# Queries and keys of a head pair in one load, and new places for the work: decay attention with a routed expert layer

## The chip, the core and the metric

The kernel runs on one core of a Trainium2 chip. A core has five engines with queues of their own: TensorE (PE, with its weight loads shown apart as PEld), VectorE (DVE), ScalarE (ACT), GpSimd (POOL) and SyncE (SP), which here only issues transfers; sixteen DMA engines do the moving. The metric is device time in microseconds (us) of one execution. Before the change three executions took 407.04, 410.15 and 414.75 us, a median of 410.15.

## The reference

Eight batches of eight heads, 576 positions, 64 numbers per head. The first stage is causal attention with a decay made of cumulated gates `f`; the second sends the 128 best-scored rows of each batch through a two-layer expert network and adds the result to them.

```python
def _attn_ref(q, k, v, f):
    scale = 1.0 / np.sqrt(D)
    scores = scale * np.matmul(q, k.transpose(0, 1, 3, 2))
    cum = np.cumsum(np.log(np.clip(f, 0.0001, 1.0)), axis=-1)
    decay = cum[:, :, :, None] - cum[:, :, None, :]
    scores = np.where(causal, -1000000000.0, scores + decay)
    attn = np.exp(scores - np.max(scores, axis=-1, keepdims=True))
    attn = attn / (np.sum(attn, axis=-1, keepdims=True) + 1e-09)
    return np.matmul(attn, v)

def _moe_ref(x, w_gate, w1, w2, capacity):          # x: (8, 576, 512), capacity 128
    scores = np.einsum('bsd,d->bs', x, w_gate)
    out = x.copy()
    for b in range(B):
        top_idx = np.argpartition(-scores[b], capacity)[:capacity]
        xe = x[b, top_idx]
        ye = np.maximum(xe @ w1, 0.0) @ w2
        g = 1.0 / (1.0 + np.exp(-scores[b, top_idx]))
        out[b, top_idx] = x[b, top_idx] + g[:, None] * ye
    return out
```

## The kernel before, in words

The 64 heads are worked in 32 pairs, two heads on the two halves of the 128 partitions. For a pair `p`:

- SyncE loads the keys of both heads (`rk`, 288 KB, one transfer, line 535) and the queries (`rq`, three transfers of 144, 128 and 16 KB, lines 540 to 542). The queries of the second head stand in another order: the last 64 first, then the others, and the first 64 of that second part are repeated at the end, so that any block of 128 columns can be taken as weights. A row of the decay (`e`, 288 KB, broadcast from DRAM) is loaded for each head (line 556) and the values (`v`, four transfers, line 606).
- GpSimd makes masked copies `m` of `e` (line 455). TensorE makes the scores of five groups of columns ("scores", line 644); VectorE adds `m` or `e` and takes the row's extreme in the same instruction (line 688); ScalarE takes the exponential (line 736); TensorE turns the result block by block ("transposes", line 755), and the turned blocks are copied out of PSUM into `pt` (line 382 on ScalarE, line 386 on VectorE); TensorE multiplies `pt` with `v` ("output products", line 838); the result is copied to `both` (the same lines 382 and 386), turned back (line 902) and normed on VectorE (line 907).
- At the end of four pairs a batch is stored, its 128 rows are selected (lines 1049, 1057, 1081), gathered by GpSimd (line 1093) and multiplied with the two layers on TensorE ("expert products", lines 1164, 1171, 1223, 1231); GpSimd scatters the rows back (line 1242).

Two kinds of copy can go to either engine. The last four copies into `pt` of a pair (blocks of 64x256, 128x256, 64x256 and 128x128) go to VectorE for the pairs in the list `ON_H`, else to ScalarE. The copy of 128x448 into `both` goes to VectorE for the pairs in `ON_O`, else to ScalarE.

The order on each engine is fixed when the program is built: a planner (class `Flow`) keeps a clock for each engine, takes the ready step that can start first, and breaks ties by the step's `place`, a number made of the constants that stand at the head of the kernel function. Every engine then runs its list in that order. A step also takes buffers: three `raw` buffers for keys and three `rq` buffers for queries, so a pair's load waits until TensorE is through with the scores of the pair three before. The transfers of SyncE use eight semaphores in turn (`DMAHW0` to `DMAHW7`), and each transfer waits at its issue for the one that used its semaphore before: at most eight are under way.

## Time and profile before

| what | value |
|---|---|
| median of 3 executions | 410.15 us (407.04 to 414.75) |
| the profiled execution's own time | 406.7 us |
| its span, first to last instruction | 405.0 us |
| TensorE busy (matmul) | 385.0 us, 95% |
| TensorE weight loads busy | 263.9 us, 65% |
| VectorE busy | 300.7 us, 74% |
| ScalarE busy | 314.0 us, 78% |
| GpSimd busy | 208.4 us, 51% |
| bytes moved | 68.06 MB, mean 168 GB/s |

The span and busy times are of one profiled execution, 3.4 us under the median of the three runs. Busy shares are means over very different stretches: a fill of some 60 us in which transfers are dense, a middle in which all engines work, and a tail of expert products from 359 us on with TensorE nearly alone.

### The profile page before, as it was taken

Reading aid. Unit: us, or ns where it says so; the run is one execution under the profiler, and the core shown is the slowest. Engines: PE = TensorE matmul, PEld = TensorE weight load, DVE = VectorE, ACT = ScalarE, POOL = GpSimd, SP = SyncE. Lnnn points to the kernel's source line nnn. Section 1 sums busy time; section 2 is a strip of 40 time slices with the busy share of each in tenths; the row PEclk is TensorE's granted clock in tenths of the full one; section 3 lists DMA queues with packets and bytes.
Section 4 is the critical chain, followed back from the end, with each engine's and each line's share of the span. In section 5 each row is a group of like instructions: output and inputs, shape, how many; then the busy total and the mean of one; then the engine's idle time right before and its main releaser. Section 6 shows DMA issues by size and latency. Waiting matters only on the chain.

```text
span 405.0 us, 11830 instructions
## 1 busy us (share of the span) xinstructions
PE 385.0 (95%) x3979; PEld 263.9 (65%) x3979; DVE 300.7 (74%) x1147; ACT 314.0 (78%) x971; POOL 208.4 (51%) x355
## 2 busy tenths in 40 slices
PE   8689898999989999999999999999999999999994
PEld 6475566656565666666675767757576657767773
DVE  3837889797995799899479963889879797278401
ACT  4979799989988998789999885689988798512220
POOL 5873778959495955337542641556453644031201
PEclk9959999999999999999999999999999999999998
DMA  5889799779888965658675651668556333011101
GB/s 146 250 212 236 197 268 247 214 204 247 239 201 260 255 182 157 201 150 246 165 203 156 177 174 45 177 200 223 159 169 187 93 120 109 34 58 54 54 0 52
DMA packets 74306, 68.06 MB, mean 168 GB/s; under 512 B 45155, under 2 KB 54406, under 8 KB 74246
## 3 DMA queue, kind: packets, MB, share of 16 engines
q1 hardware_dynamic: 72886, 62.97, 56.9%
q0 software_dynamic: 1280, 4.20, 3.0%
q8 instruction: 31, 0.51, 0.5%
q14 instruction: 29, 0.24, 0.2%
q10 hardware_dynamic: 80, 0.15, 0.1%
HBM read 55.59 MB, written 11.70 MB: 166 GB/s over the span
## 4 chain that ended last, share of the span: by engine, by line
PE 57%; DMA 12%; issue 11%; DVE 9%; ACT 6%; POOL 2%; SPq 1%; POOLq 0%; ACTq 0%; DVEq 0%
PE banks L644 15%; PE banks L838 15%; PE banks L755 8%; PE banks L1164 6%; PE banks L1223 5%; DVE p L688 4%; DMA v<-in_v_dram 4%; ACT p L736 3%; DMA rq<-in_qk_dram 3%; PE banks L1171 2%; DMA e<-eq 2%; PE banks L1231 2%; PE banks L902 2%; DMA xe<-out_dram,idx 2%; ACT pt L382 2%
## 5 line engine op out<-in xcount | busy, mean ns | idle before, releaser
L736 ACT ACTIVATE p<-p,nm 128x320 f32<-128x320 f32 (+4 forms) x288 | 166.4, 585 | 10.7 <-DVE nm L688 9.6
L455 POOL TENSOR_SCALAR_AFFINE_SELECT m<-e 128x320 f32<-128x320 f32 (+3 forms) x256 | 109.6, 457 | 83.6 <-DMA e<-eq 46.5
L382 ACT COPY pt<-banks 128x256 f32<-128x256 f32 (+4 forms) x296 | 111.8, 439 | 21.7 <-PE banks L755 20.4
L644 PE MATMUL banks<-rk,rq 64*128 64x192 f32 (+4 forms) x768 | 114.3, 417 | 3.5 <-DMA rq<-in_qk_dram 1.4
L688 DVE CUSTOM_DVE_ANT_0 p<-banks,m 64x64 f32<-64x64 f32 (+3 forms) x256 | 101.6, 418 | 12.8 <-PE banks L644 8.3
L838 PE MATMUL banks<-pt,v 128*64 128x448 f32 (+4 forms) x768 | 93.2, 392 | 0.1
L644 PEld LDWEIGHTS banks<-rk,rq 64*128 64x128 f32 x768 | 67.8, 190 | 22.5 <-DVE nm L688 6.4
L755 PEld LDWEIGHTS banks<-ident,p 64*128 64x128 f32 x1472 | 61.2, 141 | 27.3 <-issue 8.3
L838 PEld LDWEIGHTS banks<-pt,v 128*64 128x64 f32 x768 | 45.8, 137 | 47.5 <-issue 31.7
L755 PE MATMUL banks<-ident,p 64*128 64x64 f32 x1472 | 69.7, 230 | 6.9 <-ACT pt L382 4.0
L916 POOL TENSOR_TENSOR gj<-x,wg 128x640 f32<-128x640 f32 x32 | 49.9, 1568 | 35.0 <-DVE x L907 18.2
L736 ACT ACTIVATION_READ_ACCUMULATOR p<-p,nm 128x1 f32 x288 | 56.5, 196 | 0.0
L688 DVE CUSTOM_DVE_ANT_0 p<-banks,e 128x384 f32<-128x384 f32 x64 | 34.5, 552 | 14.0 <-PE banks L644 13.3
L1049 DVE SCALAR_TENSOR_TENSOR j<-srow,sg,later 128x576 uint8<-128x576 f32 (+1 forms) x40 | 33.0, 826 | 0.8
L907 DVE TENSOR_TENSOR x<-banks,rn 128x640 f32<-128x640 f32 x32 | 25.6, 816 | 9.8 <-PE banks L902 8.6
L688 DVE DVE_READ_ACCUMULATOR2_ANT nm<- 128x1 f32 (+1 forms) x384 | 31.0, 81 | 0.0
L1242 POOL DMA_INDIRECT out_dram<-xe,idx x8 | 8.7, 1086 | 40.7 <-DVE xe L1238 35.8
L921 DVE TENSOR_REDUCE gu<-gj 128x5 f32<-128x640 f32 x32 | 25.6, 813 | 4.8 <-POOL gj L916 4.8
L688 DVE CUSTOM_DVE_ANT_0 p<-banks,m,nm 128x192 f32<-128x192 f32 x64 | 26.4, 413 | 3.1 <-PE banks L644 2.3
L1223 PE MATMUL banks<-w2h,hth 128*128 128x512 f32 x64 | 27.2, 425 | 0.2 <-ACT hth L1204 0.2
L1164 PE MATMUL banks<-w1h,xth 128*128 128x512 f32 x64 | 27.0, 423 | 0.0
L1177 ACT ACTIVATE h<-banks 128x512 f32<-128x512 f32 x16 | 9.4, 596 | 22.0 <-PE banks L1171 19.8
(87 smaller groups left out, 389.9 us busy)
## 6 DMA issues: line engine op xcount, KB each, us to landing
e<-eq SPq DMA_DIRECT2D x62, 288.0 KB
rk<-in_qk_dram SPq DMA_DIRECT2D x32, 288.0 KB
out_dram<-x SPq DMA_DIRECT2D x16, 512.0 KB
rq<-in_qk_dram SPq DMA_DIRECT2D x32, 144.0 KB
rq<-in_qk_dram SPq DMA_DIRECT2D x32, 128.0 KB
v<-in_v_dram SPq DMA_DIRECT2D x32, 128.0 KB
v<-in_v_dram SPq DMA_DIRECT2D x32, 80.0 KB
srow<-sd SPq DMA_DIRECT2D x7, 320.0 KB
```

The costliest lines, as they stand in the source:

```text
L382: nc.scalar.copy(d, s_)
L455: nc.gpsimd.affine_select(out=dst, in_=src, pattern=w, compare_op=ALU.is_ge, fill=NEG, base=base, channel_multiplier=1)
L644: nc.tensor.matmul(st["sc", u][hh][:, o:o + k1 - k0], q_rows(raws["q", p], hh, i), raws["k", p][rows, k0:k1], start=True, stop=True)
L688: nc.vector.tensor_tensor_reduce(out=into(hh, i, r_, x0, x1), in0=blocks(b_[r_, x0 - k0:x1 - k0], hh, i), in1=blocks(in1(), hh, i), scale= ...
L736: nc.scalar.activation(x, x, AF.Exp, bias=st["nm", hh, i], scale=-1.0, accum_out=l)
L755: nc.tensor.transpose(tp[:, g, col:col + R], src, ident[g * R:g * R + R, g * R:g * R + R])
L838: nc.tensor.matmul(avb[p, g][par * D:(par + 1) * D, qo + q0 - g * SPL:qo + q1 - g * SPL], vt[:, j, par * D:(par + 1) * D], pt[:, off:off + ...
L907: nc.vector.tensor_tensor(out=xhs[key][:, :, w_ * P:(w_ + 1) * P].rearrange("p c (h d) -> p c h d", h=2), in0=st["tb"][:, :, 0:NCH * D].re ...
L916: (nc.vector if e == "dve" else nc.gpsimd).tensor_tensor(out=gjs[p % 2], in0=xhs[key][:, :, w0:w1], in1=wg[:, hb * HB + w0:hb * HB + w1].u ...
L1049: nc.vector.scalar_tensor_tensor(junk[0:n, :], st["srow"][0:n, 0:S], sg()[0:n, c:c + 1], later[0:n, o:o + S], ALU.subtract, ALU.is_gt, acc ...
L1164: nc.tensor.matmul(q["hp", n][0:nr, :], q["xth"][:, c, 0:nr], r_[:, c, cs], start=(c == 0 and k_ == 0), stop=False)
L1223: nc.tensor.matmul(q["yp"][0:nr, :], q["hth"][:, c, 0:nr], r_[:, c, :], start=(c == 0 and k_ == 0), stop=False)
```

## The change

Keys and queries of a pair are loaded by one transfer of 576 KB into one `raw` buffer of 1216 columns (queries, then 64 columns, then keys), and a second transfer of 16 KB repeats the first 64 queries of the second head's reordered row behind them. The `rq` buffers and the three memsets that cleared a corner of them are gone; the corner now holds the last 64 queries, which no result uses. The lists of copies on VectorE grow, `ON_H` from 6 to 15 pairs and `ON_O` from 14 to 19, and most of the planner's constants have other values. The number and the shapes of TensorE's instructions are the same.

```diff
-    ON_H = (2, 4, 6, 15, 23, 27)
-    ON_O = (0, 1, 2, 3, 4, 5, 7, 9, 12, 18, 21, 23, 29, 30)
-    BD = 18.628
+    ON_H = (0, 1, 2, 3, 5, 10, 12, 13, 14, 19, 21, 24, 25, 26, 30)
+    ON_O = (0, 1, 3, 4, 5, 8, 10, 12, 13, 14, 18, 20, 21, 22, 24, 25, 26, 29, 30)
+    BD = 17.596
...
-    PR = -837.457
-    PL = -228.901
-    PS = 1729.975
+    PR = -648.646
+    PL = -211.77
+    PS = 1838.312
...
     QW = S + R
-    RQ = 3
-    rqs = [const.tile([P, QW], F32, name=f"rq{r}") for r in range(RQ)]
...
-    def t_zero(e):
-        for t in rqs:
-            (nc.vector if e == "dve" else nc.gpsimd).memset(t[D:P, 0:R], 0.0)
-
-    d_zero = add({"dve": 0.4}, t_zero, place=-70)
-
...
-        tk = tks[p] = {"q": Token("rq", 4), "k": Token("raw", 4)}
-
-        def t_k(e):
-            t = raws["k", p] = rawp.tile([P, S], F32, tag="raw", name=f"rk{p}")
-            src = qk[2 * p:2 * p + 2, :, 1, :].rearrange("h d s -> (h d) s")
-            nc.sync.dma_start(out=t, in_=src)
-
-        def t_q(e):
-
-            t = raws["q", p] = rqs[p % RQ]
-            nc.sync.dma_start(out=t[0:D, 0:S], in_=qk[2 * p][:, 0, :])
-            nc.sync.dma_start(out=t[D:P, R:S], in_=qk[2 * p + 1][:, 0, R:S])
+        tk = tks[p] = {"k": Token("raw", 4)}
+
+        def t_qk(e):
+            t = raws[p] = rawp.tile([P, QW + S], F32, tag="raw", name=f"qk{p}")
+            x = t[:, 0:1]
+            nc.sync.dma_start(out=bass.AP(t.tensor, x.offset, [x.ap[0], [QW, 2], [1, S]]), in_=qk[2 * p:2 * p + 2].rearrange("h d g s -> (h d) g s"))
             nc.sync.dma_start(out=t[D:P, S:QW], in_=qk[2 * p + 1][:, 0, 0:R])
 
-        lk = load(t_k, 288, after=[st_eq] * (p > 1), place=pl, take=[tk["k"]])
-        lq = load(t_q, 288, 3, after=[d_zero] + [st_eq] * (p > 1), place=pl + 0.1, take=[tk["q"]])
-
-        ops[p] = [lk, lq]
+        lk = load(t_qk, 592, 2, after=[st_eq] * (p > 1), place=pl, take=[tk["k"]])
+
+        ops[p] = [lk]
...
-                        nc.tensor.matmul(st["sc", u][hh][:, o:o + k1 - k0], q_rows(raws["q", p], hh, i), raws["k", p][rows, k0:k1],
+                        nc.tensor.matmul(st["sc", u][hh][:, o:o + k1 - k0], q_rows(raws[p], hh, i), raws[p][rows, QW + k0:QW + k1],
                                          start=True, stop=True)
```

Because every place is new, instructions move on all engines. Three spots matter below; in the rows a name's first number is the pair (`rk2`, `rq2` and `qk2` are pair 2's, except that `rq` counts its three buffers) and `nm1_2_1` belongs to pair 1.

SyncE in the fill, before: twelve transfers after the keys of pair 2 have been issued (the wait in brackets is the semaphore of the transfer eight places ahead, and the engines that must be through with the buffer).

```order
L556 DMA e0_89<-eq_79 128x576 [waits DMAHW4_49,DVE_49,Pool_49]
L556 DMA e1_90<-eq_79 128x576 [waits DMAHW5_49,DVE_49,Pool_49]
L606 DMA v2_115<-in_v_dram 128x4x64 [waits DMAHW6_49]
L606 DMA v2_115<-in_v_dram 64x64 [waits DMAHW7_49]
L606 DMA v2_115<-in_v_dram 64x5x64 [waits DMAHW0_49]
L606 DMA v2_115<-in_v_dram 64x4x64
L931 DMA wg_85<-in_w_gate_dram 128x512 [waits DMAHW2_49]
L973 DMA wst0_305<-in_w1_dram 128x1024 [waits DMAHW3_49]
L556 DMA e2_91<-eq_79 128x576 [waits DMAHW4_49,DVE_49,Pool_49]
L540 DMA rq2_88<-in_qk_dram 64x576 [waits DMAHW5_49]
L541 DMA rq2_88<-in_qk_dram 64x512 [waits DMAHW6_49]
L542 DMA rq2_88<-in_qk_dram 64x64 [waits DMAHW7_49]
```

The same spot now, from the first row of the decay that is loaded:

```order
L541 DMA e2_88<-eq_79 128x576 [waits DMAHW5_49]
L527 DMA qk2_209<-in_qk_dram 128x2x576
L528 DMA qk2_209<-in_qk_dram 64x64 [waits DMAHW0_49]
L541 DMA e1_87<-eq_79 128x576 [waits DMAHW1_49,DVE_49,Pool_49]
L541 DMA e0_86<-eq_79 128x576 [waits DMAHW2_49]
L591 DMA v2_112<-in_v_dram 128x4x64 [waits DMAHW3_49]
L591 DMA v2_112<-in_v_dram 64x64 [waits DMAHW4_49]
L591 DMA v2_112<-in_v_dram 64x5x64
L591 DMA v2_112<-in_v_dram 64x4x64 [waits DMAHW6_49]
L916 DMA wg_85<-in_w_gate_dram 128x512 [waits DMAHW7_49]
L541 DMA e2_88<-eq_79 128x576 [waits DMAHW0_49,DVE_49,Pool_49]
L958 DMA wst0_305<-in_w1_dram 128x1024 [waits DMAHW1_49]
```

The queries of pair 2 moved from behind values, gate and the first weights to ahead of them; the two decay rows `e0` and `e1` changed their order, and from the first values to the second loads into `v0` and `v1` (the last transfers before pair 6) SyncE's list has 35 rows where it had 45.

ScalarE at the end of the fill's first two pairs, before:

```order
L736 ACTIVATE p1_0_236,st1_100<-p1_0_236,nm1_0_1_319 128x576
L736 ACTIVATE p1_0_236,st1_100<-p1_0_236,nm1_1_1_335 128x320
L382 COPY pt0_116<-banks_78 64x4x64
L382 COPY pt0_116<-banks_78 128x2x128
L382 COPY pt0_116<-banks_78 64x4x64
L382 COPY pt0_116<-banks_78 128x2x64
L382 COPY pt1_117<-banks_78 128x4x128 x2
L382 COPY pt1_117<-banks_78 128x2x128 x2
L736 ACTIVATE p1_2_261,st1_100<-p1_2_261,nm1_2_1_351 128x448
```

and now:

```order
L721 ACTIVATE p1_0_226,st1_97<-p1_0_226,nm1_1_1_361 128x320
L721 ACTIVATE p1_0_226,st1_97<-p1_0_226,nm1_0_1_339 128x576
L380 COPY pt1_114<-banks_78 128x2x128 x2
L721 ACTIVATE p1_2_248,st1_97<-p1_2_248,nm1_2_1_393 128x448
L380 COPY pt1_114<-banks_78 128x4x128 x2
```

The four last copies of pair 0 left ScalarE's list here (they stand on VectorE now, between the last masks of pair 1 and the first scores of pair 2), and ScalarE comes to the exponentials of pair 1 that much sooner.

TensorE around the turning back of pairs 2 and 3, before (`both` is what it waits for, the copies of the output products):

```order
L838 MATMUL banks_78<-pt1_117,v0_113 64x192 x2
L755 MATMUL banks_78<-ident_81,p4_2_831 128x64 x16
L755 MATMUL banks_78<-ident_81,p40_97 128x64 x2
L755 MATMUL banks_78<-ident_81,p4_2_831 128x64
L755 MATMUL banks_78<-ident_81,p4_0_752 128x64
L755 MATMUL banks_78<-ident_81,p4_2_831 128x64
L755 MATMUL banks_78<-ident_81,p4_0_752 128x64
L902 MATMUL banks_78<-ident_81,both_112 128x64 x20
```

and now:

```order
L823 MATMUL banks_78<-pt1_114,v0_110 64x448 x4
L823 MATMUL banks_78<-pt1_114,v0_110 64x128 x2
L823 MATMUL banks_78<-pt1_114,v0_110 64x320 x2
L823 MATMUL banks_78<-pt1_114,v0_110 64x64 x2
L823 MATMUL banks_78<-pt1_114,v0_110 64x192 x2
L887 MATMUL banks_78<-ident_81,both_109 128x64 x20
L740 MATMUL banks_78<-ident_81,p4_0_756 128x64 x24
```

The turning back stood behind 22 transposes of pair 4; now it stands right behind the products whose copies it needs, and the transposes follow it.

## Rows read from the trace of the kernel before

**Rows 1.** The page's first part: busy time, share of the span, instructions.
```profile
PE 385.0 (95%) x3979; PEld 263.9 (65%) x3979; DVE 300.7 (74%) x1147; ACT 314.0 (78%) x971; POOL 208.4 (51%) x355
```
**Rows 2.** Four stretches: length, each engine's busy time, clock, DMA share, GB/s.
```profile
8.00:60.00 52.00, 45.54 (x483) 31.74 (x483) 36.96 (x171) 45.11 (x146) 36.01 (x65) 0.90 0.88 226
60.00:140.00 80.00, 75.80 (x922) 50.62 (x918) 66.83 (x266) 74.61 (x242) 61.14 (x96) 1.00 0.85 233
140.00:340.00 200.00, 198.05 (x2140) 132.87 (x2139) 164.57 (x640) 172.34 (x540) 95.28 (x163) 1.00 0.59 166
340.00:405.00 65.00, 59.46 (x430) 44.14 (x428) 29.16 (x62) 17.76 (x41) 12.24 (x10) 0.98 0.14 48
```
**Rows 3.** Stretches of 2 us in the fill: PE, PEld, DVE, ACT, POOL, clock.
```profile
16.00:18.00 2.00, 1.06 (x16) 0.62 (x14) 1.30 (x9) 2.00 (x7) 1.94 (x6) 1.00 0.93 185
18.00:20.00 2.00, 0.76 (x13) 0.63 (x13) 1.29 (x8) 2.00 (x10) 1.79 (x7) 0.96 0.95 292
...
24.00:26.00 2.00, 1.88 (x6) 1.46 (x8) 0.22 (x1) 1.95 (x8) 1.85 (x4) 0.50 0.75 186
26.00:28.00 2.00, 2.00 (x15) 1.71 (x12) 1.33 (x7) 0.00 (x0) 2.00 (x3) 0.50 0.95 289
...
30.00:32.00 2.00, 2.00 (x18) 1.51 (x16) 1.41 (x7) 1.98 (x8) 0.00 (x0) 0.98 0.78 175
```
**Rows 4.** Chain that ended last, in the fill: start, length, what.
```profile
11.89 4.74 DMA v<-in_v_dram
...
16.65 7.86 DMA rq<-in_qk_dram
...
38.41 6.45 DMA v<-in_v_dram
```
**Rows 5.** SyncE's queue in the fill: issue of pair 2's last query transfer.
```profile
17.32 0.60 SPq L542 DMA_DIRECT2D rq<-in_qk_dram  x1
```
**Rows 6.** TensorE in time: start, length, [idle before, and what ended it].
```profile
24.12 3.50 PE L644 MATMUL banks<-rk,rq 64*128 64x384 f32 x11 [1.35 <-DMA rq<-in_qk_dram]
...
40.16 1.02 PE L755 MATMUL banks<-ident,p 64*128 64x64 f32 x22
41.71 0.83 PE L902 MATMUL banks<-ident,both 64*128 64x64 f32 x20 [0.53 <-ACT both L382]
```
**Rows 7.** VectorE in time: pair 2's first scores, and a pair's last four copies.
```profile
25.78 0.56 DVE L688 CUSTOM_DVE_ANT_0 p<-banks,e 128x384 f32<-128x384 f32 x1 [4.61 <-PE banks L644]
...
43.09 1.48 DVE L386 COPY pt<-banks 64x256 f32<-64x256 f32 x4
```
**Rows 8.** Copies by shape: count, busy us, mean ns, idle before.
```profile
L382 ACT COPY pt<-banks 128x256 f32<-128x256 f32 x90 | 30.7, 382 | 9.1 <-PE banks L755 9.1
...
L382 ACT COPY pt<-banks 64x256 f32<-64x256 f32 x52 | 19.1, 368 | 0.9 <-PE banks L755 0.5
...
L382 ACT COPY both<-banks 128x448 f32<-128x448 f32 x18 | 9.4, 524 | 5.8 <-PE banks L838 5.8
...
L386 DVE COPY both<-banks 128x448 f32<-128x448 f32 x14 | 8.6, 618 | 5.8 <-PE banks L838 5.8
L382 ACT COPY pt<-banks 128x128 f32<-128x128 f32 x26 | 6.9, 266 | 0.4
```
**Rows 9.** TensorE in time: expert products, then transposes; two products later.
```profile
229.33 0.39 PE L1223 MATMUL banks<-w2l,hth 128*128 128x512 f32 x1
229.65 0.84 PE L755 MATMUL banks<-ident,p 64*128 64x64 f32 x19
...
231.76 0.40 PE L1223 MATMUL banks<-w2l,hth 128*128 128x512 f32 x1
232.00 0.40 PE L1223 MATMUL banks<-w2h,hth 128*128 128x512 f32 x1
```
**Rows 10.** Two stretches with dense VectorE work; columns as in Rows 2.
```profile
100.00:120.00 20.00, 19.29 (x234) 13.11 (x233) 19.44 (x79) 18.95 (x59) 14.24 (x22) 1.00 0.83 217
260.00:300.00 40.00, 39.56 (x435) 26.17 (x435) 32.88 (x131) 36.71 (x117) 18.37 (x36) 1.00 0.62 174
```

More of the change, by code (lines that the diff above doesn't have):

```diff
@@ L212 @@
     FR = 3 * R
-    ON_H = (2, 4, 6, 15, 23, 27)
-    ON_O = (0, 1, 2, 3, 4, 5, 7, 9, 12, 18, 21, 23, 29, 30)
-    BD = 18.628
+    ON_H = (0, 1, 2, 3, 5, 10, 12, 13, 14, 19, 21, 24, 25, 26, 30)
+    ON_O = (0, 1, 3, 4, 5, 8, 10, 12, 13, 14, 18, 20, 21, 22, 24, 25, 26, 29, 30)
+    BD = 17.596
     WP = 17
     WQ = 0
-    R0 = -51.187
-    X0 = -111.892
-    XE_ = -1130.192
-    XH_ = 221.862
-    XM_ = -523.148
-    XB_ = -6.884
-    XN_ = -497.454
-    XO_ = -420.006
-    XU_ = 1.418
-    XQ_ = 583.927
@@ L229 @@
-    XR_ = 438.027
-    XG_ = 433.66
-    PL4 = 226.946
-    GW = 48.938
-    EPS = 0.007
-    LOOK = 13
-    PR = -837.457
-    PL = -228.901
-    PS = 1729.975
-    PV = 419.503
-    PW_ = -377.929
-    PM = -181.961
-    PE_ = 150.687
-    PC = -338.491
-    PB = -208.409
-    PD = -36.514
-    VO = -2.178
+    R0 = -52.147
+    X0 = -124.883
+    XE_ = -1075.113
+    XH_ = 159.99
+    XM_ = -564.831
+    XB_ = -7.101
+    XN_ = -664.091
+    XO_ = -436.104
+    XU_ = 1.143
+    XQ_ = 636.004
@@ L246 @@
+    XR_ = 439.718
+    XG_ = 408.245
+    PL4 = 219.529
+    GW = 52.142
+    EPS = 0.0
+    LOOK = 13
+    PR = -648.646
+    PL = -211.77
+    PS = 1838.312
+    PV = 403.168
+    PW_ = -460.22
+    PM = -142.517
+    PE_ = 117.893
+    PC = -308.846
+    PB = -168.777
+    PD = -36.497
+    VO = -0.958
     VD = 1
     GD = 0.1
-    WS = 43.949
-    WD = 829.304
-    LL = 242.025
-    A0 = 12.159
-    A1 = 57.554
-    A2 = 19.879
-    A3 = -2.292
-    A4 = 139.495
-    A5 = 55.535
-    A6 = 49.92
@@ L258 @@
-    A7 = -229.773
-    M0 = -26.555
-    M1 = -15.965
-    M2 = -18.758
-    M3 = -36.076
-    M4 = 82.571
-    M5 = -295.763
-    M6 = 466.944
-    M7 = -52.0
-    N0 = 44.201
-    N1 = -67.418
-    N2 = -47.01
-    N3 = 1.415
-    N4 = 131.251
-    N5 = 167.057
-    N6 = 116.74
-    N7 = -261.773
-    WL = 163.972
-    RK = 88.355
-    RD = 3.183
-    XP = 14.83
-    GO = 31.138
-    GS = 2.047
-    GL = -334.287
+    WS = 118.216
+    WD = 752.615
+    LL = 304.571
+    A0 = 19.277
+    A1 = 52.87
@@ new lines @@
+    A2 = 18.506
+    A3 = 3.665
+    A4 = 209.607
+    A5 = 48.408
+    A6 = 28.379
+    A7 = -323.357
+    M0 = -31.531
+    M1 = -24.322
+    M2 = -4.752
+    M3 = -43.62
+    M4 = 62.42
+    M5 = -357.068
+    M6 = 390.929
+    M7 = -62.326
+    N0 = 56.704
+    N1 = -59.781
+    N2 = -71.8
+    N3 = -2.564
+    N4 = 159.49
+    N5 = 117.493
+    N6 = 70.124
+    N7 = -235.852
+    WL = 82.957
+    RK = 91.535
+    RD = 3.307
+    XP = 16.067
+    GO = 34.078
+    GS = 2.098
+    GL = -319.652
@@ L386, in copy_on @@
             nc.vector.tensor_copy(d, s_)
-    flow = Flow({"raw": 3, "rq": 3, "v": 3, "p0": 2, "p1": 2, "p4": 2, "pt": 2, "ot0": 1, "ot1": 1,
+    flow = Flow({"raw": 3, "v": 3, "p0": 2, "p1": 2, "p4": 2, "pt": 2, "ot0": 1, "ot1": 1,
                  "x": 2, "nm": 10, "h": 1, "hth": 1, "htl": 1, "xth": 1, "xtl": 1, "xe": 2, "srow": 1,
@@ L1091, in gd @@
             else:
-                q["xe"] = rawp.tile([P, S], F32, tag="raw", name=f"xe{b}_{rt}")[:, 0:DM]
+                q["xe"] = rawp.tile([P, QW + S], F32, tag="raw", name=f"xe{b}_{rt}")[:, 0:DM]
             nc.gpsimd.indirect_dma_start(
```

## The prediction

> **What bounds the kernel now.** I read the page's first part, then busy times by stretch, then the fill in steps of 2 us with the chain of waits, then the copies by shape. The page says TensorE 95% and no other engine over 78% [rows 1]. The stretches split that up [rows 2]. From 140 to 340 us TensorE idles 1.95 us of 200, so there only less TensorE work, or closer packing, can help. From 60 to 140 us it idles 4.20 us of 80 while ScalarE is busy 74.61 of 80: ScalarE paces. From 8 to 60 us it idles 6.46 us, the DMA engines are busy at 0.88, and the clock is 0.90 of full. The last 65 us are expert products on a full TensorE and a fixed end, and I find nothing changed there. What can be won lies before 140 us: 10.7 us of idle, and a low clock.
>
> The fill in detail. [...] Inside the low stretch stands the largest single wait that the change touches: TensorE starts the scores of pair 2 at 24.12, released by that pair's queries [rows 6]. Their last transfer was issued at 17.32 [rows 5] behind values, gate vector and weights. VectorE had idled 4.61 us by then [rows 7], and ScalarE idles the whole of 26 to 28 us [rows 3]. The chain of waits shows the same: transfers that follow one another from 11.89 to 44.86 us [rows 4].
>
> **The change, part by part.** TensorE's instructions keep number and shape. So I price the waits, the copies and the order.
>
> *Fill, transfers.* Two issues fewer per pair, and the queries of pair 2 come right behind its keys. From the first values to the last transfers before pair 6 SyncE has 35 transfers where it had 45; one of the ten is a decay row put off, so nine are really gone. Since at most eight are under way, fewer transfers mean more bytes under way. Upper end of the gain: if the pace is per transfer, the chain's 33.0 us over 45 transfers are 0.73 each [rows 4], nine of them 6.6 us. Lower end: nothing, if the pace is set by bytes, for which speaks a DMA share of 0.88 [rows 2] and of 0.75 to 0.95 in the low stretch [rows 3]; the bytes even grow by 16 KB a pair (0.07 us at 226 GB/s). I take what the rows show lost at this place: the 1.35 us that TensorE waited for the queries [rows 6] and the 2.00 us of ScalarE's stop behind it [rows 3], together **-3.35 us**. Next late are the decay rows: `e0` for the second head of pair 1 now follows `e1`, and the one for pair 3 follows the loads of pair 4. That keeps me from more.
>
> The trace has 6.8 us between that last issue and the start of the scores. [...]
>
> *The three memsets* on VectorE go. They ran beside the load of `f`, before anything else could start: nothing.
>
> *Copies.* One pair's last four copies cost ScalarE 0.382 + 0.266 + 2 x 0.368 = 1.38 us [rows 8], VectorE 1.48 [rows 7]; one copy of 128x448 costs 0.524 and 0.618 [rows 8]. Nine more sets and five more large copies take 15.0 us off ScalarE's 314.0 and bring 16.4 to VectorE's 300.7. Only the stretch that ScalarE paces can gain: among pairs 2 to 13 the list has six sets where it had three, and no more large copies there. That is 4.1 us off ScalarE, 3.7 with one weight cast more. VectorE at 66.83 of 80 [rows 2] has room for 4.4 more, but both engines hold TensorE's buffers. Ends 0 and -3.7, I take the middle, **-1.8**. Pairs 0 and 1 relieve ScalarE in the fill, which is in the -3.35.
>
> *Order on TensorE.* Counting the changes of kind along its list (scores, transposes, output products, expert products, small ones), I find 240 before and 276 now. From an expert product to a transpose takes 0.32 us where one to the next takes 0.24 [rows 9]: 0.08 each. 36 more are 2.9 us, or nothing where TensorE waits anyway; half, **+1.5**, because a good part of them lies in the stretch that TensorE bounds.
>
> *Turning back without cover.* In one of 16 places (pairs 2 and 3) the turning back now stands right behind the products. In the trace the transposes behind the products start at 40.16 and the turning back at 41.71, with 0.53 idle [rows 6]: 1.55 us from products to turned block, of which the transposes hid 1.02. Without them all 1.55 is idle: **+1.0**; ends 0 and +1.0.
>
> Sum: -3.35 - 1.8 + 1.5 + 1.0 = -2.65. From the profiled execution's 406.7 that is 404.0; it lay 3.4 under the median of the runs, 410.15. Carried to the median: **407.5 us**.
>
> **Rivals.**
>
> *The lost time of the fill comes back whole.* With queries early and ScalarE lighter the clock might not fall, or only briefly. Up for grabs: 6.46 + 4.20 us of idle [rows 2] and half of the 5.9 us that TensorE spent between 24 and 30 at half clock, 2.9 (rows of 24 to 28 say 3.88 of 4) [rows 3]. Less 2.2 idle between 16 and 20, when ScalarE was full and pair 2 not due, less 2.5 for order and turning back: -8.9, so **401.3**. For it: all causes sit in one stretch. Against it: DMA share 0.88. The first row gives weight loads 65% beside TensorE's 95% [rows 1]. [...]
>
> *Transfers were hidden anyway.* The pace is bytes, the fill gains nothing, and the rest cancels: -1.8 + 1.5 + 1.0 = +0.7, **410.9**. This is also the case in which merging does not do what it says: the 16 KB transfer still takes one of eight places.
>
> *VectorE becomes the bound, slower.* The place: pairs 24 to 26, whose sets and large copies all go to VectorE now and none did before. Around 260 to 300 us VectorE is busy 32.88 of 40 [rows 10]; 3 x 1.48 + 3 x 0.618 = 6.3 more make 39.2. Its 7.1 us of idle there were waits for others, and if the share of them stays at 18% the stretch takes 39.2 / 0.822 = 47.7 us, +7.7. With all changes of kind (2.9), the turning back (1.0) and ScalarE's relief (-1.8): +9.8, **420.0**. It decides once VectorE must be busy over 97% of some 20 us: at 19.44 of 20 TensorE still idled only 0.71 [rows 10]. Against it: that row, and ScalarE's own list gets 6 us shorter in the same place.
>
> **How the numbers follow.** Chances: forecast 0.46, whole fill 0.25, hidden anyway 0.13, VectorE 0.16. About 2% (8.2 us) is what a measurement of this kernel can tell from no change, so faster means under 401.9 and slower over 418.4. Most of the second case and the low edge of the first give faster 0.25; most of the VectorE case gives slower 0.14; the rest, 0.61, is within. The forecast's own ends are -3.35 - 3.25 - 3.7 = -10.3 (fill -6.6, relief -3.7, no cost of order) and 0 + 2.9 + 1.0 = +3.9, so 399.9 to 414.1. The range goes from 399 to 416: the low end takes in most of the whole-fill case, the high end the hidden one and the mild part of VectorE's; a tenth is left out on either side.
>
> **What the new profile would show.** Fill right: the scores of pair 2 start near 21 us, no longer released by queries, and the row from 26 to 28 us shows ScalarE busy. Wrong: the same chain of transfers to 45 us, with decay rows in place of queries. Copies right: ScalarE's busy time near 299 us, VectorE's near 317, TensorE's idle from 60 to 140 us under 3 us. Order: span of 140 to 340 us with TensorE full as before but about 1 us more for the same pairs. VectorE's rival: a stretch near pairs 24 to 26 with VectorE over 97% and TensorE idle by several us. The prediction is wrong in kind if TensorE's idle after 140 us grows beyond 5 us, or if the clock row never falls.

## The result and the profile after

The changed kernel takes 412.14 us (median of 20 runs, 411.28 to 416.15). The kernel before, run again beside it, takes 407.52 us (20 runs). The ratio is 1.0103, with a 95% interval of 1.0078 to 1.0129: slower by 1%, some 4.2 us, where 0.65% faster was forecast. The sign is wrong. That the time lies within the forecast's range, 399 to 416 us, says little: the range was set around a median of three runs, 410.15, and over 20 runs the kernel before takes 407.52, which is the very figure forecast for the changed one.

The profiled execution of the changed kernel took 414.5 us, 2.4 us over its median; one of before took 406.7, under its own. So of the 7.5 us between the two spans about 3 belong to these executions. A second profile of the changed kernel (run `after_again` below) spans 410.3 us and is used beside the first. Executions of one kernel fall into a faster and a slower group: all ratios here are of the faster ones, and of the profiles only e9's is of a slower one.

> The changed kernel itself once more, on the chip of these three: 412 us, ratio 1.010, and a second profile of it. All theories: the stall near 92 us is there again; what the first profile showed and this one doesn't (its time was 2.4 us over the median) is the execution's, not the kernel's.

Measured: 413.92 us, ratio 1.0140 (1.0095 to 1.0186). The stall near 92 us is there again, to the hundredth:

```profile
91.80 1.38 PE L629 MATMUL banks<-qk 64*128 64x448 f32 x4 [1.96 <-DVE nm L673]
```

The page of the changed kernel, first part (answers to [rows 1]):

```profile
span 412.5 us, 11760 instructions
...
PE 388.1 (94%) x3979; PEld 261.2 (63%) x3979; DVE 318.8 (77%) x1185; ACT 305.5 (74%) x930; POOL 213.9 (52%) x355
```

VectorE took on 18.1 us, about what the lists say; ScalarE gave up only 8.5 where 15 were expected. The copies that left ScalarE did take 15.1 us with them (its four shapes in [rows 8] add up to 66.1 us before, and to 51.0 now); the busy time counts instructions that overlap only once. The stretches (answer to [rows 2], same columns):

```profile
8.00:60.00 52.00, 45.01 (x510) 31.01 (x510) 40.98 (x176) 44.37 (x138) 35.88 (x62) 0.93 0.86 244
60.00:140.00 80.00, 73.47 (x850) 46.87 (x850) 68.27 (x268) 73.19 (x232) 61.03 (x96) 0.98 0.73 217
140.00:340.00 200.00, 197.26 (x2096) 128.99 (x2094) 170.52 (x645) 161.65 (x501) 98.45 (x163) 1.00 0.57 166
```

TensorE's idle time from 60 to 140 us grew from 4.20 to 6.53 us, and the clock there is 0.98 instead of 1.00. The fill on TensorE (answers to [rows 6]), start, length, what, and the idle time before with what ended it:

```profile
21.18 1.11 PE L740 MATMUL banks<-ident,p 64*128 64x64 f32 x15 [0.96 <-ACT pt L380]
22.04 0.95 PE L629 MATMUL banks<-qk 64*128 64x384 f32 x1
```

Pair 2's scores start at 22.04 instead of 24.12 us and wait for no transfer, and ScalarE, idle from 26 to 28 us before, is busy there for the whole 2 us. That part came. What took it back shows in TensorE's waits from 40 to 140 us (engine, line, released by: sum, times, longest). The three largest of the changed kernel:

```profile
PE banks L629 <- DVE nm L673: 3.2, 4, 2.0
PE banks L823 <- DVE nm L673: 1.3, 3, 0.5
PE banks L740 <- DVE both L384: 0.7, 2, 0.5
```

and of the kernel before:

```profile
PE banks L755 <- ACT pt L382: 2.0, 6, 0.5
PE banks L902 <- ACT pt L382: 0.9, 2, 0.6
PE banks L644 <- DVE pt L386: 0.7, 2, 0.4
```

Over all rows of that view TensorE waited 3.6 us for ScalarE and 1.8 for VectorE before, and 1.1 and 7.2 now (1.1 and 6.0 in the second profile). `nm` is what the masked scores on VectorE leave: until VectorE has read a score, TensorE has no buffer for the next. The longest of them, in the first profile:

```profile
89.07 1.09 PE L629 MATMUL banks<-qk 64*128 64x192 f32 x8
92.12 1.02 PE L629 MATMUL banks<-qk 64*128 64x448 f32 x4 [1.96 <-DVE nm L673]
92.97 0.41 PE L740 MATMUL banks<-ident,p 64*128 64x64 f32 x8
93.89 4.48 PE L823 MATMUL banks<-pt,v 128*64 128x448 f32 x24 [0.51 <-DVE nm L673]
```

VectorE in the same microseconds has batch 0's rankings in front of pair 9's first score part (L1034: five instructions that count for each row how many rows score higher; the selection of the 128 rows follows from them):

```profile
87.44 1.46 DVE L1034 SCALAR_TENSOR_TENSOR j<-srow,sg,later 128x576 uint8<-128x576 f32 x1
...
88.95 1.71 DVE L1034 SCALAR_TENSOR_TENSOR j<-srow,sg,later 128x576 uint8<-128x576 f32 x1
...
90.70 0.88 DVE L1034 SCALAR_TENSOR_TENSOR j<-srow,sg,later 128x576 uint8<-128x576 f32 x1
...
91.51 0.55 DVE L673 CUSTOM_DVE_ANT_0 p<-banks,e 128x384 f32<-128x384 f32 x1
```

Before, they stood at 104.66 to 109.2 us, behind pair 10's parts, and took 0.81 to 0.82 us each. The first of them:

```profile
104.66 0.81 DVE L1049 SCALAR_TENSOR_TENSOR j<-srow,sg,later 128x576 uint8<-128x576 f32 x1
```

The first two are 1.8 and 2.1 times as long now, and GpSimd is at work beside them, at the residual `w2l` of the expert's weights (a weight less its rounded copy `w2h`):

```profile
86.44 1.28 POOL L966 TENSOR_TENSOR w2l<-wst,w2h 128x512 fp32r<-128x512 f32 x1
...
88.38 1.66 POOL L966 TENSOR_TENSOR w2l<-wst,w2h 128x512 fp32r<-128x512 f32 x1
```

After its wait TensorE's clock falls, to 0.50 from 94 to 96 us (columns as above, stretches of 2 us):

```profile
92.00:94.00 2.00, 1.38 (x14) 0.82 (x15) 2.00 (x9) 0.52 (x2) 1.82 (x4) 0.90 0.60 150
94.00:96.00 2.00, 2.00 (x6) 0.86 (x8) 2.00 (x9) 2.00 (x8) 0.93 (x3) 0.50 0.82 225
96.00:98.00 2.00, 2.00 (x18) 1.18 (x16) 1.93 (x8) 0.84 (x3) 0.00 (x0) 0.75 0.73 243
```

The 24 output products at 93.89 take 4.48 us where those of the pair ahead, at 84.98, took 2.92.

To follow a loss through reordered lists I add up TensorE's instructions, each at the median pace of its shape, and read when each kernel has done the same sum. This is an estimate from one profile each, good to some half a us (the pace of a shape can be taken in more than one way). In us against the kernel before (minus is ahead):

| before stands at | changed | changed, 2nd profile | loads only (e1) | split loads (e4) | ranks spread (e10) | short ranks (e12) |
|---|---|---|---|---|---|---|
| 35.6 | -2.1 | -2.7 | -1.1 | -2.8 | -2.0 | -2.1 |
| 87.8 | -0.9 | -1.2 | -0.8 | -1.6 | -0.8 | -0.9 |
| 97.7 | +2.9 | +2.2 | -0.8 | +2.2 | +0.7 | -0.5 |
| 118.1 | +4.9 | +3.6 | -0.9 | +3.6 | +2.0 | +2.0 |
| 199.7 | +3.9 | +2.4 | -1.0 | +2.9 | +1.2 | +1.3 |
| 397.4 | +7.5 | +5.3 | 0.0 | +5.9 | +5.0 | +4.2 |

The largest step lies between 88 and 98 us: 3.4 to 3.8 us. The fill's gain had shrunk before it, and 3.1 to 4.6 us come later, in small steps: 1.4 to 2.0 of them by 118 us, where TensorE's waits for VectorE are 0.3 to 0.5 us each.

### The profile page after: what moved, and what is told of

Same layout as the page of the kernel before. It is cut to its first block, busy times and chain, and to the rows that moved or that the text cites. A ratio compares the mean times of both kernels' runs of the same rounds, so it can differ in the third digit from the quotient of the medians.

```text
span 412.5 us, 11760 instructions
## 1 busy us (share of the span) xinstructions
PE 388.1 (94%) x3979; PEld 261.2 (63%) x3979; DVE 318.8 (77%) x1185; ACT 305.5 (74%) x930; POOL 213.9 (52%) x355
## 3 DMA queue, kind: packets, MB, share of 16 engines
HBM read 56.12 MB, written 11.70 MB: 164 GB/s over the span
## 4 chain that ended last, share of the span: by engine, by line
PE 61%; issue 10%; DVE 10%; DMA 6%; POOL 6%; ACT 5%; POOLq 0%; SPq 0%; DVEq 0%; ACTq 0%
PE banks L823 18%; PE banks L629 15%; PE banks L740 9%; PE banks L1149 5%; PE banks L1208 5%; DVE p L673 4%; DMA xe<-out_dram,idx 3%; ACT p L721 3%; PE banks L1156 3%; POOL gj L901 2%; PE banks L1216 2%; ACT pt L380 2%; DVE j L1034 2%; PE banks L887 2%; POOL m L453 1%
## 5 line engine op out<-in xcount | busy, mean ns | idle before, releaser
L721 ACT ACTIVATE p<-p,nm 128x192 f32<-128x192 f32 (+4 forms) x288 | 166.1, 582 | 17.2 <-DVE nm L673 16.6
L453 POOL TENSOR_SCALAR_AFFINE_SELECT m<-e 128x320 f32<-128x320 f32 (+3 forms) x256 | 114.8, 477 | 80.0 <-DVE nm L673 37.2
L380 ACT COPY pt<-banks 128x512 f32<-128x512 f32 (+4 forms) x260 | 100.3, 449 | 28.5 <-PE banks L740 24.2
L629 PE MATMUL banks<-qk 64*128 64x192 f32 (+4 forms) x768 | 116.3, 417 | 5.3 <-DVE nm L673 3.9
L673 DVE CUSTOM_DVE_ANT_0 p<-banks,m 128x192 f32<-128x192 f32 (+3 forms) x256 | 101.6, 417 | 14.6 <-PE banks L629 3.7
L823 PE MATMUL banks<-pt,v 128*64 128x448 f32 (+4 forms) x768 | 94.8, 397 | 1.3 <-DVE nm L673 1.3
L629 PEld LDWEIGHTS banks<-qk 64*128 64x128 f32 x768 | 64.9, 189 | 26.7 <-DVE nm L673 13.9
L823 PEld LDWEIGHTS banks<-pt,v 128*64 128x64 f32 x768 | 47.0, 138 | 49.0 <-issue 31.6
L1034 DVE SCALAR_TENSOR_TENSOR j<-srow,sg,later 128x576 uint8<-128x576 f32 (+1 forms) x40 | 36.2, 904 | 0.9
L1208 PE MATMUL banks<-w2l,hth 128*128 128x512 f32 x64 | 25.2, 393 | 0.0
```

The lines of the kernel that those rows point to most:

```text
L380: nc.scalar.copy(d, s_)
L453: nc.gpsimd.affine_select(out=dst, in_=src, pattern=w, compare_op=ALU.is_ge, fill=NEG, base=base, channel_multiplier=1)
L629: nc.tensor.matmul(st["sc", u][hh][:, o:o + k1 - k0], q_rows(raws[p], hh, i), raws[p][rows, QW + k0:QW + k1], start=True, stop=True)
L673: nc.vector.tensor_tensor_reduce(out=into(hh, i, r_, x0, x1), in0=blocks(b_[r_, x0 - k0:x1 - k0], hh, i), in1=blocks(in1(), hh, i), scale= ...
L721: nc.scalar.activation(x, x, AF.Exp, bias=st["nm", hh, i], scale=-1.0, accum_out=l)
L823: nc.tensor.matmul(avb[p, g][par * D:(par + 1) * D, qo + q0 - g * SPL:qo + q1 - g * SPL], vt[:, j, par * D:(par + 1) * D], pt[:, off:off + ...
```

## Experiments: the parts alone

The planner answers any changed constant with new places. So each kernel here plans as one of the two kernels does, and only what the planned steps emit is changed.

**e1, the loads alone.** The kernel before, whose step for the keys now issues both transfers of the change; the step for the queries issues nothing.

```diff
         def t_k(e):
-            t = raws["k", p] = rawp.tile([P, S], F32, tag="raw", name=f"rk{p}")
...
+            t = raws[p] = rawp.tile([P, QW + S], F32, tag="raw", name=f"qk{p}")
+            x = t[:, 0:1]
+            nc.sync.dma_start(out=bass.AP(t.tensor, x.offset, [x.ap[0], [QW, 2], [1, S]]), in_=...)
+            nc.sync.dma_start(out=t[D:P, S:QW], in_=qk[2 * p + 1][:, 0, 0:R])
...
         def t_q(e):
...
+            pass
```

> The kernel before with one part of the change: its order, costs and lists stay as they were, and only the loads are merged (576 KB and 16 KB of a pair into one buffer, at the place where the keys were loaded; nothing stands any more where the three query transfers stood). Theory 1, the places: the change lost its time through the new order alone, and the loads give what the trace of after shows at the fill, 2.1 to 2.4 us; so 405.1 us, ratio to before 0.994, with pair 2's scores released near 22 us instead of 24.1. Theory 3, the loads hold nothing or cost: ratio 1.00 or above, and pair 2 starts no earlier once the order is the old one.

Measured: 408.31 us, 1.0004 (0.9975 to 1.0032). Pair 2's scores in the fill:

```profile
24.04 3.36 PE L639 MATMUL banks<-qk 64*128 64x384 f32 x12 [1.68 <-ACT pt L381]
```

They start 0.08 us earlier. The wait for queries is gone, and one for a ScalarE copy that frees the buffer stands in its place: the old order had two things due at 24 us. The 1 us of lead in the table comes behind this start (from 28 to 30 us the clock reads 0.82 here and 0.50 before) and is lost again by 278 us.

**e2, the lists alone; e3, the old lists in the new order.** The step's engine is overwritten at emission (e3 the same with the old lists, in the changed kernel):

```diff
                 def both_halves(e, cps=cps):
+                    e = "dve" if p in (0, 1, 2, 3, 5, 10, 12, 13, 14, 19, 21, 24, 25, 26, 30) else "act"
...
         def out(e):
+            e = "dve" if p in (0, 1, 3, 4, 5, 8, 10, 12, 13, 14, 18, 20, 21, 22, 24, 25, 26, 29, 30) else "act"
```

> The kernel before with another part of the change alone: order and loads as before, but the copies are put on VectorE by the new lists (15 block-0 copies instead of 6, 19 output copies instead of 14), each at its old place in the program. Theory 1, the places: within 1.5 us of before, 406 to 409 us, since TensorE waits for neither engine in most stages. Theory 2, the lists: the copies on VectorE are what costs, so most of the change's 4.2 us shows here, 411 to 412 us, with TensorE waiting for score parts (nm) of VectorE between 60 and 140 us.

> The changed kernel with the old lists: new order, new loads, but the copies go back to ScalarE wherever the lists of before had them there. Theory 1, the places: no better than the changed kernel, 411 to 414 us, and TensorE still idles near 92 us for VectorE with the ranking of batch 0 in front of it. Theory 2, the lists: back to 408 us.

Measured: e2 419.39 us, 1.0311 (1.0264 to 1.0357); e3 423.19 us, 1.0372 (1.0332 to 1.0412). Neither theory had that: each list costs about 2.7 to 3.1% in the other's order. Order and lists only fit each other; more on VectorE isn't what costs by itself, since in e3 less on VectorE costs too. How is shown at one place only, 0.87 of e2's 11 us: in its fill a pair's last copies sit on VectorE before a score part, and TensorE waits behind it (VectorE's row first, then TensorE's). That the rest is of the same kind I haven't shown:

```profile
29.85 1.43 DVE L386 COPY pt<-banks 64x256 f32<-64x256 f32 x4
```

```profile
24.38 3.39 PE L644 MATMUL banks<-rk,rq 64*128 64x384 f32 x11 [2.25 <-DMA rq<-in_qk_dram]
...
32.29 1.89 PE L644 MATMUL banks<-rk,rq 64*128 64x192 f32 x12 [0.87 <-DVE nm L688]
```

**e15, loads and lists in the old order** (both edits above).

> The kernel before with the new loads and the new lists, order as before. With the lists alone TensorE waited 2.3 us for pair 2's queries near 22 us. Theory 3b, the loads pay only where the lists have freed pair 2's buffers earlier: about 2.3 us less than with the lists alone, 417 us, ratio 1.025. Rival, the loads hold nothing in any combination: 419 us, ratio 1.031.

Measured: 417.25 us, 1.0202 (1.0147 to 1.0256), 2.1 us under e2's median, and 4.4 us by the two ratios. The 2.25 us wait for queries is gone:

```profile
23.50 3.36 PE L639 MATMUL banks<-qk 64*128 64x384 f32 x12 [0.74 <-ACT pt L381]
...
31.43 1.89 PE L639 MATMUL banks<-qk 64*128 64x192 f32 x12 [1.75 <-DVE nm L683]
```

So with these lists the loads pay, but little of it is seen: pair 2's scores start 0.88 us earlier than in e2, and 0.88 of the 1.51 us that the first wait lost goes into the next one. The two profiled executions end alike (spans of 416.2 and 416.0 us), so where the timed 2 to 4 us come from stays open.

**e4, the new order with split loads.**

```diff
-            nc.sync.dma_start(out=bass.AP(t.tensor, x.offset, [x.ap[0], [QW, 2], [1, S]]), in_=...)
+            nc.sync.dma_start(out=t[:, QW:QW + S], in_=...)
+            nc.sync.dma_start(out=t[0:D, 0:S], in_=...)
+            nc.sync.dma_start(out=t[D:P, 0:S], in_=...)
```

> The changed kernel with its loads split again: at the place of each 576 KB load stand three transfers of 288, 144 and 144 KB into the same buffer, the 16 KB one stays; order and lists as in the changed kernel. Theory 1, the places, with the loads worth 2.1 to 2.4 us at the fill: 414.3 us, ratio to before 1.016, pair 2's scores about 2 us later than in the changed kernel. Theory 3, the loads hold nothing: 412 us; if merged loads cost: 408 to 410 us.

Measured: 415.85 us, 1.0195 (1.0159 to 1.0231), beside 1.0103 and 1.0140 for the changed kernel. Yet its pair 2 starts at 21.98 us, and in its profile the fill leads by 2.8 us, as with merged loads. Theory 1's time came, its place didn't. The fill's gain thus belongs to the new order and lists, in which pair 2's loads stand earlier. What the split costs in the timed runs, 0.5 to 0.9%, its profiled execution (412.76 us, the fastest of six) doesn't show; where it falls stays open.

## Experiments: the rankings of batch 0

**e5 and e6, the rankings moved back.** The changed kernel's plan is kept as a list; named steps, and those that need them, are held behind another step, all others keep their order and their buffers. In e5 the five rankings of batch 0 are held behind pair 9's last score part (below); in e6 behind pair 10's, and the turned rows of the expert behind pair 11's.

```diff
+    HOLDS = [([('rank', 0, 0), ('rank', 0, 1), ('rank', 0, 2), ('rank', 0, 3), ('rank', 0, 4)], ('m', 9, 3, 1, 0))]
```

> The changed kernel with one thing moved, all else word for word in its order: the five rankings of batch 0 and their selection stand on VectorE behind the last score part of pair 9 instead of before and between pair 9's parts (one score and turning block of TensorE passes the gather's products in exchange). Theory 1, the places: TensorE's 1.96 us wait at 92.12 and the 0.51 us one at 93.89 go, with them the fall of the clock that follows; 4 us less than the changed kernel, 408 us, ratio to before about 1.00. Theory 4, VectorE is full between 87 and 110 us in any order: the wait only moves to pair 10's score parts, 411 to 414 us, ratio 1.01.

> As the last, but the five rankings, the selection and the gather's index go behind pair 10's last score part, where the kernel before had them, and the gathered rows are turned behind pair 11's. Theory 1: 408 us, as the last or better, since the kernel before has room there. Theory 4: the first expert's rows come some 12 us later than in the changed kernel, and the expert's products wait for them at about 123 us: 414 us or more.

Measured: e5 416.51 us, 1.0189 (1.0147 to 1.0231); e6 417.24 us, 1.0236 (1.0186 to 1.0285). Slower than the changed kernel, so theory 1 as I had put it fell. But the profile of e5 shows another cause than theory 4's:

```profile
91.67 0.46 PE L838 MATMUL banks<-ident,p 64*128 64x64 f32 x8 [0.24 <-ACT pt L475]
96.87 0.71 PE L838 MATMUL banks<-ident,p 64*128 64x64 f32 x16 [0.32 <-ACT pt L475]
102.74 0.30 PE L1169 MATMUL banks<-tok,oh 128*128 128x1 f16 x5 [4.46 <-DVE oh L1144]
```

The wait at 92 us is gone, and at 97.7 us this kernel is level with before. Then TensorE, which takes its list in order, stands 4.46 us at five products of one column that need the selection (5.21 in e6). These two tell nothing on the price of the place; the gather's products would have had to move too.

**e10, the rankings spread.** Rankings 1 and 2 are held behind pair 9's first score part, ranking 3 behind its part of 320 columns.

```diff
+    HOLDS = [([('rank', 0, 1), ('rank', 0, 2)], ('m', 9, 0, 0, 3)), ([('rank', 0, 3)], ('m', 9, 1, 0, 1))]
```

> The changed kernel with three of batch 0's rankings moved by one or two places on VectorE: the second and third behind the first score part of pair 9 instead of before it, the fourth behind the 320-wide part; all other orders untouched. Theory 4 with the rankings' place as the trigger: TensorE's 1.96 us wait near 92 us shrinks below 0.7 us, the fall of the clock behind it does not come, and the run is 1.5 to 2.5 us shorter than the changed kernel, 410.5 us, ratio 1.007. Rival, VectorE has too much to do there in any order: waits of the same sum appear at 93 to 100 us, 412 to 413 us, ratio 1.011 to 1.013.

Measured: 411.14 us, 1.0084 (1.0054 to 1.0113), 1 to 2.8 us under the changed kernel's two medians; the intervals overlap, so the times alone don't show a gain. The profile shows the stall gone: the wait of 1.96 us is no more, the next one is 0.78, and the clock from 92 to 98 us reads 1.00 where it was 0.72:

```profile
91.22 0.46 PE L838 MATMUL banks<-ident,p 64*128 64x64 f32 x8 [0.24 <-ACT pt L475]
92.45 2.99 PE L921 MATMUL banks<-pt,v 128*64 128x448 f32 x24 [0.78 <-DVE nm L770]
...
92.00:98.00 6.00, 5.31 (x69) 3.89 (x71) 5.93 (x21) 5.27 (x16) 3.38 (x7) 1.00 0.81 222
```

**e12 and e13, the rankings cut short,** in the changed kernel and in the one before. Batch 0's expert gets other rows than the reference's.

```diff
+            m = S if b else R
-            ... st["srow"][0:n, 0:S], sg()[0:n, c:c + 1], later[0:n, o:o + S], ...
+            ... st["srow"][0:n, 0:m], sg()[0:n, c:c + 1], later[0:n, o:o + m], ...
```

> The changed kernel with batch 0's five rankings cut to 64 of 576 columns, so that their ranks, and the rows that batch 0's expert takes, are not the reference's; the index is held below 576 in the instruction that converts it. Orders, loads and lists are the changed kernel's. An estimate from the ranking's 0.82 us and from copies of 64 columns (0.23 us): 5.9 us of VectorE become 1.2. Theory 4, VectorE has no room left between 87 and 110 us: 3.5 to 5 us less than the changed kernel, 408 us, ratio to before about 1.00, and no fall of the clock near 93 us. Rival, the stall near 92 us is made up later (VectorE's chain is late anyway): under 1.5 us.

> The kernel before with the same cut of batch 0's rankings, which there stand at 104.7 to 109 us behind pair 10's parts. Theory 4: they lie in room that the kernel before has, so 0 to 1.5 us less, ratio 0.997 to 1.000. Rival, the rankings cost their length in any place: 3 us less or more, ratio 0.993, and then their place is not what tells the two kernels apart.

Measured: e12 410.66 us, 1.0055 (1.0022 to 1.0087); e13 407.55 us, 0.9982 (0.9950 to 1.0014). In the kernel before the rankings are hidden, to 0.2% in the middle and 0.5% at the interval's end. In the changed kernel they cost 1.5 to 3.3 us, the difference to its two medians, a third to more than a half of what it lost; e12's interval still touches that of the changed kernel's first measurement (1.0078 to 1.0129), so this size is loose. The profile is plainer: the wait near 92 us is 0.53, and the clock stays at 1.00. Some of the gain goes again: e12 loses 2.5 us from 98 to 118 us (table), more than the changed kernel.

```profile
90.68 1.02 PE L629 MATMUL banks<-qk 64*128 64x448 f32 x4 [0.53 <-DVE nm L673]
```

VectorE's rankings there:

```profile
87.43 0.93 DVE L1035 SCALAR_TENSOR_TENSOR j<-srow,sg,later 128x64 uint8<-128x64 f32 x1
...
88.41 1.33 DVE L1035 SCALAR_TENSOR_TENSOR j<-srow,sg,later 128x64 uint8<-128x64 f32 x1
...
89.78 0.36 DVE L1035 SCALAR_TENSOR_TENSOR j<-srow,sg,later 128x64 uint8<-128x64 f32 x1
```

A ninth of the columns, and still 1.33 us beside GpSimd's residual (88.38 to 89.66), against 0.36 right behind it. The length isn't in the columns: the ranking ends at 89.74, 0.08 us behind the residual.

**e7 and e11, GpSimd made to wait.** One copy of one column, which reads the third ranking, ahead of GpSimd's residual, which is held behind that ranking; e11 also holds the fourth ranking as e10 does.

```diff
+    HOLDS = [([('wl', 6), ('wh', 7), ('wl', 7)], ('rank', 0, 2))]
...
+            if b == 0 and c == 2:
+                nc.gpsimd.tensor_copy(pick[:, 0:1], rk[:, 2:3])
```

> The changed kernel with one tiny copy added on GpSimd: it reads the third ranking of batch 0, so that GpSimd's residual of the weights and the masks behind it start only when three of the five rankings are done; every other instruction keeps its place on every engine. [...]

> The kernel with GpSimd waiting for the third ranking, and the fourth ranking moved behind pair 9's 320-wide part, where GpSimd is at its masks. [...]

Measured: e7 412.97 us, 1.0105 (1.0065 to 1.0146); e11 413.44 us, 1.0149 (1.0117 to 1.0180). The lengths change with the overlap in e7: the first three rankings, which were 1.46, 1.71 and 0.88 us, take 0.81, 0.82 and 0.82, the residual 1.27 instead of 1.66, and TensorE's wait is 0.36:

```profile
90.57 1.02 PE L726 MATMUL banks<-qk 64*128 64x448 f32 x4 [0.36 <-DVE nm L770]
...
93.03 2.99 PE L921 MATMUL banks<-pt,v 128*64 128x448 f32 x24 [1.19 <-DVE nm L770]
```

The time follows little or not at all: the intervals of e7 and of the changed kernel overlap. The fourth ranking now meets the residual (1.78 us), and the wait comes 2.5 us later. In e11 the fourth ranking takes 0.81 us and that wait goes, but GpSimd, held back by some 2 us, brings its masks late; VectorE waits for them, and TensorE for VectorE (VectorE's row first):

```profile
95.45 0.42 DVE L770 CUSTOM_DVE_ANT_0 p<-banks,m,nm 128x192 f32<-128x192 f32 x1 [0.81 <-POOL m L548]
```

```profile
96.35 0.27 PE L838 MATMUL banks<-ident,p 64*128 64x64 f32 x1 [1.22 <-DVE nm L770]
```

So the two engines do lengthen each other here (1.78 us for 0.81, 1.66 for 1.27). What that costs in time these two runs can't tell, since each pays for it with a late GpSimd.

## Experiments: what a block on VectorE costs

**e8, e9 and e14: five added instructions** in the kernel before, at pair 8, at pair 20, and one behind each of pairs 18 to 22.

```diff
+                if p == 8 and i == 0 and hh == 1:
+                    for c in range(5):
+                        nc.vector.scalar_tensor_tensor(junk[:, 0:512], wg, tok32[:, 0:1], later[:, 0:512], ...)
```

> The kernel before, with five instructions of the ranking's kind added on VectorE behind pair 8's last score part, the place where the changed kernel has batch 0's rankings. They compute nothing that is used (512 wide, the gate's weights and the order table as sources, results to a scratch buffer); an estimate from the rankings' 0.82 us at 576 wide is 0.74 us each, 3.7 us. Theory 4, VectorE has no room left around there: at least half of it shows, 2 to 4 us, ratio to before 1.005 to 1.010, with TensorE waiting for score parts near 90 us. Rival, the place alone was never the matter: under 1 us, since VectorE of the kernel before is idle 2.7 us of the 10 us from 90 to 100 us.

> The same five added instructions behind pair 20's last score part, in the kernel before, where VectorE is busy 15.0 of 24.6 us. Theory 4: hidden, below 1 us, ratio 1.000 to 1.002. Rival, in-order VectorE passes any 3.7 us on to TensorE wherever they stand: 2 to 4 us, as at pair 8.

> The kernel before with five added VectorE instructions as at pair 20, but one behind the last score part of each of pairs 18 to 22. Theory 6, TensorE is reached by the length of one block in VectorE's order, since VectorE's slack before the next score part is some 1 us a pair: under 1.5 us, ratio below 1.004, no wait of TensorE over 1 us. Rival, the sum counts: 4 to 6 us, as in one block.

Measured: e8 413.88 us, 1.0143 (1.0108 to 1.0179); e9 416.11 us, 1.0194 (1.0144 to 1.0244); e14 410.26 us, 1.0066 (1.0022 to 1.0109). I had expected nothing at pair 20, and it cost no less than at pair 8. My 15.0 of 24.6 us did not hold for the place: the kernel before has that only from 224.4 us on (14.96), and right behind the place VectorE works 9.22 of 9.40 us (columns as above; VectorE is the third):

```profile
212.41:221.81 9.40, 9.40 (x111) 5.39 (x108) 9.22 (x33) 8.40 (x28) 2.63 (x7) 1.00 0.55 158
```

So no run here puts a block where VectorE has room behind it. TensorE behind the block, of e8 and then of e9:

```profile
95.21 4.56 PE L843 MATMUL banks<-pt,v 128*64 128x448 f32 x24 [2.62 <-DVE nm L688]
```

```profile
224.13 5.28 PE L843 MATMUL banks<-pt,v 128*64 128x448 f32 x24 [4.60 <-DVE nm L688]
```

Five instructions of 0.75 to 0.93 us, from 89.39 to 93.86 in e8, cost 5.8 to 6.2 us: TensorE runs dry, and then takes 4.56 and 5.28 us for products that usually take 2.92; the clock in e8 reads 1.00 from 94 to 96 us and 0.61 from 96 to 98, and in e9 its mean from 140 to 340 us is 0.98, in the kernel before 1.00. e9's profiled execution is a long one, 419.71 us: of the 13.0 us that its span has over the kernel before, 6.0 are lost before the block and 7.0 at it, by the sums used for the table. The same five, a pair apart, cost 2.4 to 2.7 us; the longest wait in their stretch is 0.66, and at the place of e9's block, where one of them stands, it is 0.60:

```profile
190.03 1.02 PE L644 MATMUL banks<-rk,rq 64*128 64x448 f32 x4 [0.66 <-DVE nm L688]
...
215.01 2.92 PE L842 MATMUL banks<-pt,v 128*64 128x448 f32 x24 [0.60 <-DVE nm L688]
```

e14's middle, about half a microsecond for each piece, lies between the two sides of its expectation, and its interval (0.9 to 4.4 us) reaches both. That the block costs more than its pieces is clear of the noise: e9's interval and e14's don't meet. No run here breaks an instruction up; e14 only sets whole ones apart.

## Why the prediction was wrong

**Fill, transfers, -3.35.** The size was near, 2.1 to 2.7 us at 36 us, and that is luck, since the cause was not. The loads alone gain 0.08 us at pair 2 and nothing in the end (e1), and with split loads the new order has the whole lead (e4). I read one releaser, the queries [rows 6], and did not ask what else was due at that time; ScalarE's copy was, 0.1 us ahead of them. The sum also took one delay twice: ScalarE's stop of 2.00 us, which it adds to TensorE's 1.35, was ended by TensorE itself, behind pair 2's late scores:

```profile
28.84 0.86 ACT L382 COPY pt<-banks 128x384 f32<-128x384 f32 x2 [2.89 <-PE banks L755]
```

The rival that the transfers were hidden anyway was right for the loads by themselves in the old order; in the new one the merged loads are worth 0.5 to 0.9% in the timed runs (e4), at a place that I haven't found. The lead was then mostly given back between 46 and 88 us, to waits for VectorE, which no term covered.

**Copies, -1.8.** This step failed. I took what ScalarE is relieved of for a gain, because ScalarE was 93% busy from 60 to 140 us [rows 2], and called VectorE's 84% room. Relief came: TensorE's waits for ScalarE fell by 2.5 us. Its waits for VectorE rose by 4.2 to 5.4, and its idle time from 60 to 140 us, forecast to fall under 3 us, rose to 6.53. Busy share is a mean: over the whole run VectorE is at 74% [rows 1], and yet behind e9's place it works 9.22 of 9.40 us, and five instructions there cost more than their length. What the copies cost apart from the order no run tells, since lists and order can't be taken apart (e2, e3).

**Order, +1.5.** Here is the largest single loss, and the term priced the wrong thing. I counted changes of kind on TensorE and did not look at what the new order puts ahead of the scores on VectorE. The five rankings moved by 17 us, from behind pair 10 to before pair 9, and both lists of VectorE showed that before any run. From 88 to 98 us the changed kernel loses 3.4 to 3.8 us; in the first profile the wait of 1.96 and the slow products (4.48 for 2.92, so 1.56) are 3.5 of them. Cutting the rankings took most of this step away (e12: 0.4 us lost there), and 1.5 to 3.3 us of the time. Nor could the early rankings pay: the expert's first product still began at 122.90 us, 1.8 earlier than before, although its gathered rows were turned 12.5 us earlier (108.80 for 121.29).

**Turning back, +1.0.** The row at 41.71 that I priced it from [rows 6] is of pairs 0 and 1. Pairs 2 and 3 are turned back at 60.4 us before, with no wait, and now at 56.12 right behind the products: the first half without a wait, the second after 0.26 us. Too much by 0.7.

```profile
60.48 0.78 PE L902 MATMUL banks<-ident,both 64*128 64x64 f32 x19
```

```profile
56.12 0.53 PE L887 MATMUL banks<-ident,both 64*128 64x64 f32 x10
56.90 0.52 PE L887 MATMUL banks<-ident,both 64*128 64x64 f32 x10 [0.26 <-DVE both L384]
```

**VectorE as the bound, given 0.16.** That TensorE would come to wait for VectorE was right; the place was wrong, and so was what fills VectorE, rankings and not copies. At pairs 24 to 26 nothing happened: from 260 to 300 us TensorE is busy 40.00 of 40 and VectorE 29.58, less than before [rows 10], since those pairs moved too. I set its threshold by share (97% over 20 us). Around the stall VectorE is busy 18.59 of the 20 us from 84 to 104 us, 93%: one block of 4 us was enough.

**The clock.** I expected the fill's low stretch to shorten; it did: the rows read 0.50 from 20 to 30 us before, and 0.62, 0.50, 0.50 and 0.67 from 18 to 26 us now. The second low stretch, behind the new wait, makes up for it: between 8 and 100 us each kernel spends some 10 us at a clock of 0.50, an estimate from the rows of 2 us, in which a reading between 0.50 and 1.00 is taken as a mix of the two.

**Open.** Some 3 us between 140 us and the end come in steps of about 1 us near 210, 270 and 340 us; TensorE idles 2.74 us instead of 1.95 from 140 to 340 us. One of these steps is of the same kind as the stall, work placed ahead of what it needs; it stands in both profiles:

```profile
335.79 0.28 PE L1066 MATMUL banks<-tok,oh 128*128 128x1 f16 x5 [1.04 <-DVE oh L1042]
```

The rest is perhaps in the pace from one kind to the next; I have no run that tells whether that is the order's. So of the 4.2 to 5.6 us lost, the runs show the cause of 1.5 to 3.3. No version beat the kernel before: e10 is the best of the new order, and e1 and e13 equal it.

## What to carry to other kernels

Before an engine is given more work because its busy share has room, look at what stands in its list ahead of the instruction that the critical engine waits for; a block of 4 us of work that nobody needs yet cost 6 to 8 us here, in front of a dense stretch, and the same work in five pieces 2.5. A wait that a change removes is worth only the time to the next thing due at the same place, so list all releasers there, not the last one. Lists and orders that were chosen together are one change: either half of this one, put with the other's old half, ran 2.0 to 3.7% slower than the kernel before (e2, e3, e15).
